# The stores of the gates and of the tokens' order move into the branch of the general path

## The chip, the cores and the metric

The kernel runs on one core of a Trainium2 chip. The metric is the device time of one execution in microseconds (us). TensorE (PE in the rows) multiplies matrices, VectorE (DVE), ScalarE (ACT) and GpSimd (POOL) work on tiles, and SyncE (SP) issues most of the DMAs. Each engine has a sequencer of its own (PEq, DVEq, ACTq, POOLq, SPq) that runs its stream of instructions; PEld stands for TensorE's weight loads.

## The reference

Three layers in a row, all with float32 inputs and outputs. A decay attention of 2 x 8 heads, 768 positions and head size 64 gives 1536 rows `x` of 512. A mixture of 8 experts follows, in which each row goes to one expert:

```python
logits = x @ w_gate
expert_idx = np.argmax(logits, axis=1)
...
gate_w = probs[np.arange(N), expert_idx]
...
    h = np.maximum(xe @ w1[e], 0.0)
    ye = h @ w2[e]
    out[mask] = gate_w[mask, None] * ye
```

Here `w1[e]` is 512 x 1024 and `w2[e]` 1024 x 512. A gated layer ends it, with 1536 inner columns: `sigmoid(x @ w_gate) * (x @ w_val) @ w_out`.

## The kernel before, in words

Every float32 matrix of the two later layers is split into two float16 halves (`hi` and `lo`), and a product is three float16 matmuls. The stages follow one another in the program:

1. Attention, with routing woven into it (lines 264 to 666). Twelve blocks of 128 rows; each block's rows are also stored to DRAM (`rows_d`). The routing gives for every token its expert (`oh_all`), its rank in the expert (`rank_all`) and its gate (`gt_all`, final at some 81 us).
2. The experts (lines 814 to 868). The eight experts are sorted by their token counts, and expert `e` is computed for a fixed number of tokens, `W[e]` of line 47. Its rows are gathered from `rows_d`, multiplied by the gate, transposed and multiplied by `w1` (L827) and `w2` (L855). The result goes into `yh` and `yl`, in order of experts (L863, L864).
3. `order` (line 743, called once at line 869, behind the last expert). TensorE makes a list that holds at each place the token that stands there (L746), and VectorE copies it to `oidx` (L747). SyncE stores the gates to `gate_d` in two DMAs (L749, one for each batch) and `oidx` to `list_d` (L751).
4. The general path (lines 876 to 932). It is for experts with more tokens than `W[e]`. `further` (line 753) counts how many more rounds each expert needs; the largest count is read into a register of every engine at line 842 (`mxv`), and `tc.If(mxv > 0)` at line 876 runs two nested loops. In them GpSimd loads pieces of `list_d` (L885, L886) and gathers rows from `rows_d` and gates from `gate_d`, and TensorE multiplies in float32. Nothing else reads `gate_d` and `list_d`.
5. The gated layer (lines 935 to 980). `gv_ps` (L956) holds `x @ w_gate` and `x @ w_val` in turn, 864 matmuls of 512 columns; sigmoid, product and split follow on ScalarE and VectorE (L960 to L965); `o_ps` (L975) multiplies by `w_out`. GpSimd writes the rows to their tokens' places by the list in SBUF, `oidx` (L979).

The order is written out by hand: the tile framework is told not to reorder (`manual_schedule`), so each engine runs its instructions as the program issues them, and only the semaphores are put in by the framework. Weights of the gated layer come by SyncE in pieces of 1 MB into two buffers (`wload`, L150). Each is turned from its double-precision words to float32 and split, one small step at a time, wherever the program calls `work64`; the next piece can be loaded once VectorE has read the buffer (L219). The If is no part of this order: the framework treats its body as a block, and each engine meets the branch in its own stream.

Of the kernel before, what the change touches and what calls it, by code (L numbers as in the profile page):

```python
# [32 lines left out]
def kernel(  # L33
# [15 lines left out]
    nc = tc.nc  # L49
    B, H, S, D = q.shape  # L50
# [3 lines left out]
    L = 128  # L54
# [41 lines left out]
    gt_all = const.tile([128, NT, 1], F32, name="gt_all")  # L96
    acc = const.tile([128, E], F16, name="acc")
    gidx = const.tile([128, 2, E], I32, name="gidx")
    oidx = const.tile([128, NT], I32, name="oidx")
# [4 lines left out]
    gate_d = dram.tile([NTOK, 1], F32, name="gate_d")  # L104
    list_d = dram.tile([NTOK, 1], I32, name="list_d")
# [141 lines left out]
    def bank(kind, shape, name):  # L247
        turns[kind].append(turns[kind].pop(0))
        tag, bufs = turns[kind][-1]
        return ps.tile(shape, F32, tag=tag, bufs=bufs, name=name)  # L250
# [13 lines left out]
    with ExitStack() as actx:  # L264
# [366 lines left out]
        t = NT - 2  # L631
# [42 lines left out]
    with ExitStack() as mctx:  # L674
# [68 lines left out]
        def order(P, R):  # L743
            ops = bank("b", [128, NT], "o_idx")
            for t in range(NT):
                nc.tensor.matmul(ops, lhsT=P[:, t], rhs=R[:, t], start=(t == 0), stop=(t == NT - 1))  # L746
            nc.vector.tensor_copy(oidx, ops)  # L747
            for b in range(B):
                nc.sync.dma_start(out=gate_d[b * S:(b + 1) * S, :].rearrange("(k p) o -> p k o", p=L),  # L749
                                  in_=gt_all[:, b::B])  # L750
            nc.sync.dma_start(out=list_d[:, :].rearrange("(t p) o -> p (t o)", p=128), in_=oidx)  # L751

        def further():

# [59 lines left out]
        for e in range(E):  # L814
# [31 lines left out]
            for dp in range(KD // 2):  # L846
# [19 lines left out]
                if e < E - 1 or dp == 0:  # L866
                    weights()
            freed[0] = 4 * e + 3
        order(*PR)

    ectx.close()


    with ExitStack() as octx:
        ox_p = octx.enter_context(tc.tile_pool(name="ox", bufs=1))
        with tc.If(mxv > 0):  # L876
            with tc.For_i(0, E, 1) as e:
                nxe = nc.values_load(tab[0:1, bass.ds(e + 2 * E, 1)], min_val=0, max_val=NTOK)
                end = nc.values_load(tab[0:1, bass.ds(e + E, 1)], engines=(ET.DVE, ET.Activation, ET.Pool),
# [2 lines left out]
                with tc.For_i(0, nxe, 1) as i:  # L882
# [6 lines left out]
                    for r, n in ((0, 128), (1, CO - 128)):  # L889
                        nc.gpsimd.indirect_dma_start(  # L890
                            out=xg[0:n, r, :], out_offset=None, in_=rows_d[:, :],
                            in_offset=IndirectOffsetOnAxis(ap=wi[0:n, r:r + 1], axis=0))
                        nc.gpsimd.indirect_dma_start(
                            out=gw[0:n, r:r + 1], out_offset=None, in_=gate_d[:, :],
# [23 lines left out]
                    for dp in range(KD // 2):  # L918
                        w = ox_p.tile([128, KF, 256], F32, tag="ow", name="ow2")
                        nc.gpsimd.dma_start(  # L920
                            out=w, in_=moe_w2[bass.ds(eo, 1), :, dp * 256:(dp + 1) * 256].rearrange(
                                "o (f p) d -> p (o f) d", p=128))
# [12 lines left out]
    with ExitStack() as gctx:  # L935
# [7 lines left out]
        for a in range(KF2 // 4):  # L943
            wg, wv = NC1 + 2 * a, NC1 + 2 * a + 1
            for c2 in range(2):
                for g in range(NG):
                    ts = slice(g * 512, (g + 1) * 512)
                    for f in range(4 * a + 2 * c2, 4 * a + 2 * c2 + 2):
                        fs = slice((f % 4) * 128, (f % 4) * 128 + 128)
                        banks = []  # L950
                        for w in (wg, wv):
                            need(w, c2)
                            p = bank("a", [128, 512], "gv_ps")
# [14 lines left out]
        for t in range(NT):  # L968
            tsl = slice(t * 128, (t + 1) * 128)
            op = bank("b", [128, DM], "o_ps")  # L970
            for f in range(KF2):
# [8 lines left out]
                out=out, out_offset=IndirectOffsetOnAxis(ap=oidx[:, t:t + 1], axis=0), in_=osb, in_offset=None)  # L980
# [30 lines left out]
```

## Time and profile before

| | |
|---|---|
| median of 3 runs | 529.22 us (529.05, 529.22, 531.6) |
| the profiled execution | 530.62 us |
| its span, first to last instruction | 529.0 us |
| TensorE busy in it | 506.9 us (96%) |
| VectorE, ScalarE, GpSimd busy | 306.7, 222.5, 68.3 us |
| TensorE's granted clock, mean | 0.984 |
| DMA | 72.29 MB in 70592 packets, 43338 of them under 512 B |

All times within the execution are counted from the start of the span. [...] "L876" is line 876 of the kernel. A busy time of TensorE contains the pipelining of its matmuls, so that groups overlap. The 16 DMA engines serve several queues: q1 carries what SyncE issues, q0 what GpSimd issues, q8 and q14 carry code for the engines.

### The profile page before, as it was taken

To read this page: it belongs to the slowest core of one execution; us is meant where nothing else is said; L and a number is where in the kernel's file an instruction comes from. 1 tells how busy PE (TensorE), PEld (TensorE's weight loads), DVE (VectorE), ACT (ScalarE), POOL (GpSimd) and SP (SyncE) were. 2 spreads that over 40 slices of the span, in tenths; PEclk is the share of its full clock that TensorE was granted. 3 is DMA by queue.
4 is the path that set the end of the run, shared out by engine and by line. 5 is a ranking of instruction groups with operands and counts; after the bars stand their busy time and mean duration, and the time that the engine had idled before them with its cause. 6 is when DMAs were issued, how large, how long until landed. Compare 5 with 4: busy or idle time off the path is not lost.

```text
span 529.0 us, 9790 instructions
## 1 busy us (share of the span) xinstructions
PE 506.9 (96%) x4013; PEld 340.5 (64%) x4014; DVE 306.7 (58%) x505; ACT 222.5 (42%) x328; POOL 68.3 (13%) x78
## 2 busy tenths in 40 slices
PE   7999998999999999957999999999999999999995
PEld 6888877999999999953444444444444444444442
DVE  5556867979977987741777757677766620000000
ACT  3554642865876787430343433443344310000000
POOL 3676403301200100000000000000000001101101
PEclk9999999999999999987999999999999999999998
DMA  9999865775989885240233222342231001011011
GB/s 171 215 245 268 270 232 184 237 272 168 338 281 314 280 274 187 83 82 1 79 111 128 81 79 81 95 145 79 81 110 51 0 1 40 21 40 41 24 37 40
DMA packets 70592, 72.29 MB, mean 137 GB/s; under 512 B 43338, under 2 KB 43338, under 8 KB 70544
## 3 DMA queue, kind: packets, MB, share of 16 engines
q1 hardware_dynamic: 68192, 65.05, 41.1%
q0 software_dynamic: 2208, 6.57, 3.6%
q8 instruction: 33, 0.54, 0.5%
q14 instruction: 15, 0.12, 0.1%
q10 hardware_dynamic: 144, 0.00, 0.0%
HBM read 65.31 MB, written 6.30 MB: 135 GB/s over the span
## 4 chain that ended last, share of the span: by engine, by line
PE 52%; issue 1%; DMA 1%; POOLq 0%; ACT 0%; ACTq 0%
PE gv_ps L956 36%; PE o_ps L975 16%; DMA out_dram<-osb,oidx 1%; POOLq L1006 0%; ACT osb L978 0%; ACTq L978 0%; POOLq L979 0%
## 5 line engine op out<-in xcount | busy, mean ns | idle before, releaser
L956 PEld LDWEIGHTS <-hi 128*128 128x128 f16 x576 | 56.6, 98 | 77.6 <-issue 10.6
L171 DVE SCALAR_TENSOR_TENSOR lo<-st,hi 128x1024 f16<-128x1024 f32 x64 | 77.9, 1234 | 13.5 <-ACT hi L170 13.3
L956 PE MATMUL gv_ps<-yh,hi 128*128 128x512 f16 x288 | 74.7, 382 | 8.8 <-PEq L876 8.8
L956 PE MATMUL gv_ps<-yh,lo 128*128 128x512 f16 x288 | 74.8, 382 | 0.0
L956 PE MATMUL gv_ps<-yl,hi 128*128 128x512 f16 x288 | 74.4, 381 | 0.0
L170 ACT ACTIVATE hi<-st 128x1024 f16<-128x1024 f32 x64 | 66.2, 1053 | 3.5 <-DMA st<-in_moe_w_dram 3.4
L855 PE MATMUL y_ps<-hl,hi 128*128 128x224 f16 (+6 forms) x256 | 64.6, 253 | 0.3 <-DVE hl L831 0.3
L855 PE MATMUL y_ps<-hh,hi 128*128 128x224 f16 (+6 forms) x256 | 64.6, 253 | 0.0
L855 PE MATMUL y_ps<-hh,lo 128*128 128x224 f16 (+6 forms) x256 | 64.6, 253 | 0.0
L979 POOL DMA_INDIRECT out_dram<-osb,oidx x12 | 11.7, 974 | 336.0 <-ACT osb L978 336.0
L975 PE MATMUL o_ps<-hi,uh 128*128 128x512 f16 x144 | 54.6, 379 | 0.0
L975 PE MATMUL o_ps<-lo,uh 128*128 128x512 f16 x144 | 54.6, 379 | 0.0
L975 PE MATMUL o_ps<-hi,ul 128*128 128x512 f16 x144 | 54.6, 379 | 0.0
L964 ACT CAST uh<-u 128x512 f16<-128x512 f32 x36 | 22.2, 618 | 70.4 <-DVE u L963 70.4
L956 PEld LDWEIGHTS <-lo 128*128 128x128 f16 x288 | 28.4, 99 | 34.6 <-issue 1.1
L975 PEld LDWEIGHTS <-uh 128*128 128x128 f16 x288 | 28.2, 98 | 34.0
L855 PEld LDWEIGHTS <-hi 128*128 128x128 f16 x512 | 47.7, 98 | 0.2
L827 PEld LDWEIGHTS <-hi 128*128 128x128 f16 x512 | 46.4, 98 | 1.2 <-issue 1.1
L978 ACT ACTIVATE osb<-o_ps 128x512 f32<-128x512 f32 x12 | 7.2, 597 | 85.3 <-PE o_ps L975 85.3
L963 DVE SCALAR_TENSOR_TENSOR u<-gv_ps,sg 128x512 f32<-128x512 f32 x36 | 24.7, 687 | 30.2 <-PE gv_ps L956 25.2
L965 DVE TENSOR_TENSOR ul<-u,uh 128x512 f16<-128x512 f32 x36 | 24.9, 692 | 24.6 <-ACT uh L964 24.6
L827 PE MATMUL h_ps<-xh,hi 128*128 128x224 f16 (+6 forms) x256 | 33.5, 253 | 0.3 <-ACT xh L706 0.2
(168 smaller groups left out, 712.6 us busy)
## 6 DMA issues: line engine op xcount, KB each, us to landing
st<-in_moe_w_dram SPq DMA_DIRECT2D x64, 512.0 KB, 5.6
st<-in_moe_w_gate_dram SPq DMA_DIRECT2D x6, 1024.0 KB, 5.3
st<-in_moe_w_val_dram SPq DMA_DIRECT2D x6, 1024.0 KB, 5.1
st<-in_moe_w_out_dram SPq DMA_DIRECT2D x6, 1024.0 KB, 4.9
q<-in_q_dram SPq DMA_DIRECT2D x12, 256.0 KB, 4.5
k<-in_k_dram SPq DMA_DIRECT2D x12, 256.0 KB, 4.9
v<-in_v_dram SPq DMA_DIRECT2D x12, 256.0 KB, 5.9
rows_d<-X SPq DMA_DIRECT2D x12, 256.0 KB, 4.1
```

The costliest lines, as they stand in the source:

```text
L170: nc.scalar.activation(out=hi, in_=w, func=AF.Copy, scale=SW)
L171: return lambda: nc.vector.scalar_tensor_tensor(out=lo, in0=w, scalar=SW, in1=hi, op0=ALU.mult, op1=ALU.subtract)
L827: nc.tensor.matmul(hp[:, j], lhsT=lw[w][:, c, fs], rhs=rx[:, c], start=(c == 0 and m == 0), stop=(c == KD - 1 and m == 2))
L855: nc.tensor.matmul(yp[:, j], lhsT=lw[w][:, f % 4, ds], rhs=rh[:, f], start=(f == 0 and m == 0), stop=(f == KF - 1 and m == 2))
L956: nc.tensor.matmul(p, lhsT=lw[w][:, c, fs], rhs=ry[:, c, ts], start=(c == 0 and m == 0), stop=(c == KD - 1 and m == 2))
L963: nc.vector.scalar_tensor_tensor(out=u, in0=banks[1], scalar=SU, in1=sg, op0=ALU.mult, op1=ALU.mult)
L964: nc.scalar.copy(uh[:, f, ts], u)
L965: nc.vector.tensor_tensor(ul[:, f, ts], u, uh[:, f, ts], op=ALU.subtract)
L975: nc.tensor.matmul(op, lhsT=lu[:, f, tsl], rhs=rw[w][:, f % 4, :], start=(f == 0 and m == 0), stop=(f == KF2 - 1 and m == 2))
L978: nc.scalar.activation(out=osb, in_=op, func=AF.Copy, scale=1.0 / (SX * SW * SW * SY * SW * SU * SW))
L979: nc.gpsimd.indirect_dma_start(out=out, out_offset=IndirectOffsetOnAxis(ap=oidx[:, t:t + 1], axis=0), in_=osb, in_offset=None)
```

## The change

Four lines leave the end of `order` and stand, unchanged, at the start of the If's body. `oidx` is still made in `order`.

```diff
             nc.vector.tensor_copy(oidx, ops)
-            for b in range(B):
-                nc.sync.dma_start(out=gate_d[b * S:(b + 1) * S, :].rearrange("(k p) o -> p k o", p=L),
-                                  in_=gt_all[:, b::B])
-            nc.sync.dma_start(out=list_d[:, :].rearrange("(t p) o -> p (t o)", p=128), in_=oidx)
...
         with tc.If(mxv > 0):
+            for b in range(B):
+                nc.sync.dma_start(out=gate_d[b * S:(b + 1) * S, :].rearrange("(k p) o -> p k o", p=L),
+                                  in_=gt_all[:, b::B])
+            nc.sync.dma_start(out=list_d[:, :].rearrange("(t p) o -> p (t o)", p=128), in_=oidx)
             with tc.For_i(0, E, 1) as e:
```

## Rows read from the trace of the kernel before

**Rows 1.** The chain that ended last, in order of time: start, us, what.

```profile
241.10 0.19 issue
241.30 188.72 PE gv_ps L956 x864
```

**Rows 2.** TensorE's waits, whole span: us in total, times, longest.

```profile
PE gv_ps L956 <- PEq L876: 8.8, 1, 8.8
```

**Rows 3.** Timeline 230.5 to 262: start, us, engine, line; in brackets idle before.

```profile
232.02 0.45 PE L746 MATMUL o_idx<-R,P 128*128 128x12 f16 x12
...
232.73 0.54 DVE L864 SCALAR_TENSOR_TENSOR yl<-y_ps,yh 128x368 f32 x1 [1.27 <-ACTq L876]
...
241.30 1.86 PE L956 MATMUL gv_ps<-yh,hi 128*128 128x512 f16 x4 [8.83 <-PEq L876]
...
246.17 0.60 ACT L960 ACTIVATE sg<-gv_ps 128x512 f32<-128x512 f32 x1 [12.00 <-PE gv_ps L956]
```

**Rows 4.** Line 876: ns min/median/max, then first and last start in us.

```profile
L876 POOLq EVENT_SEMAPHORE  x5: 17/43/43, 175.9 to 182.6; - x5
...
L876 PEldq COMPARE_BRANCH  x1: 9262/9262/9262, 231.6 to 231.6; - x1
L876 ACTq COMPARE_BRANCH  x1: 45/45/45, 232.2 to 232.2; - x1
L876 DVEq COMPARE_BRANCH  x1: 72/72/72, 232.7 to 232.7; - x1
L876 SPq COMPARE_BRANCH  x1: 53/53/53, 233.8 to 233.8; - x1
```

**Rows 5.** DMA queues, 233.3 to 233.5: packets that start there, MB, share of 16 engines.

```profile
q8 instruction: 1, 0.02, 124.7%
```

**Rows 6.** DMA queues, 180 to 200.

```profile
q8 instruction: 2, 0.03, 0.6%
```

**Rows 7.** DMA queues, whole span.

```profile
q8 instruction: 33, 0.54, 0.5%
```

**Rows 8.** DMA packets, 228 to 245.

```profile
DMA packets 3651, 1.10 MB, mean 65 GB/s; under 512 B 3136, under 2 KB 3136, under 8 KB 3648
```

**Rows 9.** Windows: length, five engines' busy us, granted clock, DMA share, GB/s.

```profile
230.00:232.50 2.50, 2.47 (x40) 2.37 (x37) 1.46 (x3) 0.83 (x2) 0.00 (x0) 1.00 0.97 359
...
236.00:239.50 3.50, 0.00 (x0) 0.00 (x0) 0.00 (x0) 0.00 (x0) 0.00 (x0) 0.50 0.28 1
239.50:241.00 1.50, 0.00 (x0) 0.00 (x0) 0.00 (x0) 0.00 (x0) 0.00 (x0) 0.50 0.04 0
...
235.00:235.50 0.50, 0.00 (x0) 0.00 (x0) 0.00 (x0) 0.00 (x0) 0.00 (x0) 0.80 0.19 1
...
245.50:246.00 0.50, 0.50 (x4) 0.25 (x3) 0.00 (x0) 0.00 (x0) 0.00 (x0) 0.95 0.00 0
...
74.88:78.29 3.41, 2.75 (x47) 2.53 (x44) 1.32 (x10) 2.07 (x5) 0.00 (x0) 1.00 0.26 97
78.29:81.70 3.41, 3.40 (x47) 3.32 (x47) 2.46 (x19) 2.21 (x3) 1.17 (x1) 0.50 0.00 1
```

**Rows 10.** SyncE's DMA issues, 150 to 300: start, us.

```profile
228.16 0.38 SPq L150 DMA_DIRECT2D st<-in_moe_w_val_dram  x1
228.59 1.09 SPq L749 DMA_DIRECT2D gate_d<-gt_all  x2
...
254.10 0.37 SPq L150 DMA_DIRECT2D st<-in_moe_w_gate_dram  x1
264.44 0.37 SPq L150 DMA_DIRECT2D st<-in_moe_w_val_dram  x1
```

**Rows 11.** SyncE's waits, 228 to 262: us in total, times, longest.

```profile
SPq L150 <- DVE cv L219: 39.4, 3, 19.9
```

**Rows 12.** Line 877, the general path's outer loop.

```profile
nothing on L877; most used: ['L956', 'L827', 'L855', 'L975', 'L395', 'L380', 'L409', 'L443', 'L150', 'L361', 'L340', 'L391', 'L171', 'L701', 'L454', 'L563', 'L170', 'L960', 'L963', 'L293', 'L524', 'L352', 'L863', 'L964', 'L965']
```

**Rows 13.** DMA queues, 241.7 to 245: packets that start there.

```profile
q8 instruction: 1, 0.02, 5.6%
```

## The prediction

> **What bounds the kernel now.** I read the chain that ended last first. It is TensorE alone: gv_ps from 241.30 for 188.72 us and then o_ps, and it begins at 241.10, in the middle of the program, with a gap in front of it [rows 1]. TensorE's waits name that gap: 8.8 us before the first gv_ps matmul, put down to TensorE's own sequencer at L876, the If [rows 2]. So from 241.30 on every microsecond by which TensorE starts earlier is a microsecond off the end, if its operands are there.
>
> The timeline shows who is busy in the gap [rows 3]. TensorE's twelve o_idx matmuls begin at 232.02 and take 0.45, so it is idle from 232.47 to 241.30. Its operands are ready early: the last yl is written at 232.73 + 0.54 = 233.27, and ACT stands idle for 12.00 us before its first sigmoid at 246.17, so from 234.17 on, waiting for gv_ps. Nothing that computes holds TensorE.
>
> The rows of L876 show what does [rows 4]: one compare-and-branch that takes TensorE's sequencer 9262 ns from 231.6, to about 240.85. ACT, DVE and SP branch in 45 to 72 ns, in the same microseconds. So it is no barrier of all engines, and TensorE's branch has a cost that theirs have not. The DMA view says what it is. In 233.3 to 233.5 one packet of instructions (16 KB) starts, and it is put at 124.7% of 16 engines' 0.2 us, so it takes 1.247 x 3.2 = 3.99 us, to about 237.4 [rows 5]. The two that fell in 180 to 200, beside weight loads at 298 GB/s, took 0.006 x 16 x 20 / 2 = 1.0 us each [rows 6], and the mean of all 33 is 0.005 x 16 x 529 / 33 = 1.3 us [rows 7]. TensorE jumps over the general path's matmuls, has to load code, and that load takes three to four times as long as usual.
>
> Beside it lie the stores. From 228 to 245, 3136 packets are under 512 B [rows 8]; the two gate stores (768 words each) and the list store (1536) make 3072 of them, 4 bytes each. The windows show their tail [rows 9]: 359 GB/s up to 232.5 is the 1 MB weight load issued at 228.16, but in 236 to 239.5 the DMA engines are 0.28 busy at 1 GB/s, and from 239.5 only 0.04. TensorE's branch comes free just behind that tail. The clock adds to the gap: granted 0.80 in the half microsecond from 235.0, so it falls within it, 0.50 after, and 0.95 in the half that ends at 246.
>
> **The change, part by part.** (1) SP loses two gate stores (1.09 us of issue, from 228.59 on), the wait for oidx and the list store [rows 10]. Worth nothing by itself: SP's next load goes out at 254.10, after 19.9 us of waiting for DVE [rows 11], and no engine waits for the stores. Nothing but code is queued behind them, for the next data transfer is that of 254.10.
>
> (2) The three stores go into a path that isn't run (no instruction of its loop at L877 shows [rows 12]), so none of their 3072 packets is sent. What they take from TensorE's code load is the term that counts. Without them the wait has three pieces, each bounded:
> - From the branch (231.6) to the packet's start: at most the present 233.4 - 231.6 = 1.8 us; at least some 0.9, since the code packet that follows the present branch's end at 240.85 starts behind 241.7, in a quiet stretch [rows 13]. The 1 MB load is still in flight to about 232.5, so I take 1.4.
> - The packet: 1.0 to 1.3 us [rows 6, 7]; I take 1.0, the two that lay beside weight loads, as this one does.
> - From the packet's end to the branch's: now 240.85 - 237.4 = 3.4 us, with the stores' tail beside it. That is the upper end; the lower is nothing. I take 0.4, since the tail that fills it now is gone.
>
> Sum 2.8 us, with ends at 0.9 + 1.0 = 1.9 and 1.8 + 1.3 + 3.4 = 6.5. To the first matmul come the present 241.30 - 240.85 = 0.45 us. So TensorE starts at 231.6 + 2.8 + 0.45 = 234.85 and **gains 6.45 us** (ends: 7.35 and 2.75). yl at 233.27 is ready before even the early end; ACT is free from 234.17, and its first sigmoid comes now 4.87 us behind TensorE's start. DVE, ACT and SP's loads behind 241 follow TensorE's results, and move with it.
>
> [...]
>
> (3) The clock. [...] With an idle time of 234.85 - 232.47 = 2.4 us the clock either doesn't fall (gain 2.1) or falls as late as it did (gain nothing). The nearest rows: it fell after 2.5 to 3 us of idling here, and by 78.29 even in a stretch with TensorE busy 2.75 of 3.41 us, where the row at 0.50 is 3.41 us long [rows 9]. 2.4 is near the first, so I take a fall, with the price of such a row: 3.4 us at half speed lose 1.7. **Gain 0.4 us** (ends 0 and 2.1).
>
> (4) Added: SP has to square its semaphores on the path not taken, and its branch jumps further. What that costs is seen on POOL, whose DMAs already stand in the If: five semaphore instructions from 175.9 to 182.6, spread over 6.7 us [rows 4]. SP, at its branch by 228.59 + 1.09 = 229.7 even with the gate stores' issue, would be done by 236.4 at the upper end; at the lower end it adds a few short instructions. The cover is the wait up to 254.10, which moves to 247.3: 10.9 us remain. If they didn't suffice, the weight loads would be late next. I take nothing.
>
> Sum: 6.45 + 0.4 = 6.85 us. The profiled execution, 530.62 with a span of 529.0, would take 523.8; it was 1.4 above the median of 529.22, so for the median I say **522.4**.
>
> **Rivals.**
> - *The clock stays up* (chance 0.20): 6.45 + 2.1 = 8.6 us, 520.6. For it: at 235.0 it had not fallen yet, and TensorE is back by then. Against it: the fall by 78.29, with TensorE at work.
> - *The wait is the branch's own* (0.13): the slow packet and the late end come with a jump, and the stores only lie beside them. Then 241.30 stays, and 529.2, or at best some 2 us less. For it: ACT's and SP's branches, among the same stores, take no time, so stores alone delay no branch; and the packet after the branch, when the small packets are over, still took 0.056 x 16 x 3.3 = 3.0 us [rows 13]. Against it: the two of 180 to 200, and the small packets, which thin out at 239.5, just ahead of the branch's end. [...]
> - *SP's bookkeeping holds the weights* (0.04): if SP's counts on the path not taken are squared only behind something later than the landings, its next load is late. It decides from 247.3 on; loads go out 10.3 us apart (254.10, 264.44), so a whole one missed costs 10.3 - 6.85 = 3.5 us: 532.7, slower. Against it: POOL's took 6.7 us, and SP has 17.6.
>
> **How the numbers follow.** The forecast, a start at 234 to 236.5 with a fall of the clock, has 0.63. A measurement of this kernel tells some 0.5% (2.6 us) from no change. Forecast and the first rival are both faster by more; so faster 0.83, the branch's own wait is same, 0.13, SP's is slower, 0.04. The range: downwards the early start without a fall, 7.35 + 2.1 = 9.45, about 519.8; upwards a start at 237.0 with a fall as dear as now, 4.3 us, 524.9. This leaves out the two last rivals and the latest starts, some 0.2.
>
> **What would show it.** Right: L876's branch on TensorE takes 2 to 4 us; the code packet in it some 1 us; no crowd of packets under 512 B between 232 and 240; the wait before gv_ps is 2 to 3.5 us; SP's loads behind 240 are all earlier by the same amount. The granted clock behind 235 decides between forecast and first rival. Wrong: a branch still near 9 us without those packets; a new wait of gv_ps on DVE or a DMA, with SP's load later than 254.

## The result, and the profile after

| | before | after |
|---|---|---|
| median | 530.94 us (13 runs) | 523.29 us (13 runs) |
| lowest, highest | 527.7, 535.63 | 521.39, 527.42 |
| span of the profiled execution | 529.0 us | 521.7 us |
| TensorE's idle time in front of gv_ps | 8.83 us | 3.03 us |
| TensorE's branch at the If | 9262 ns | 3462 ns |

The kernel after is faster: the ratio is 0.9869, with a 95% interval of 0.9844 to 0.9893. One execution of a kernel further down (gates outside) took 667.47 us at a mean granted clock of 0.747; the ratios leave it out. Line 876 of before is line 872 of after.

The rows of that line in the kernel after, with ns min/median/max and first and last start in us:

```profile
L872 SPq EVENT_SEMAPHORE  x4: 17/17/17, 228.1 to 228.4; - x4
L872 SPq COMPARE_BRANCH  x1: 53/53/53, 227.9 to 227.9; - x1
L872 PEldq COMPARE_BRANCH  x1: 3462/3462/3462, 230.9 to 230.9; - x1
L872 ACTq COMPARE_BRANCH  x1: 45/45/45, 231.6 to 231.6; - x1
L872 DVEq COMPARE_BRANCH  x1: 72/72/72, 232.1 to 232.1; - x1
```

Against [rows 4] only TensorE's branch has changed. SP meets the If at 227.9 in place of 233.8, as it no longer waits for oidx, and squares its counts with four instructions of 17 ns: three more than before, done by 228.4.

TensorE's wait in front of gv_ps, from its waits (us in total, times, longest):

```profile
PE gv_ps L956 <- PEq L872: 3.0, 1, 3.0
```

The beginning of the chain that ended last:

```profile
234.65 0.19 issue
234.84 187.94 PE gv_ps L956 x864
```

Two rows of the timeline, the last matmuls ahead of the gap and the first behind it:

```profile
231.37 0.45 PE L746 MATMUL o_idx<-R,P 128*128 128x12 f16 x12
...
234.84 1.87 PE L956 MATMUL gv_ps<-yh,hi 128*128 128x512 f16 x4 [3.03 <-PEq L872]
```

The span's 7.3 us can be laid out with these and [rows 1, 3]. The o_idx matmuls begin 232.02 - 231.37 = 0.65 us earlier, which is scatter of the work ahead (the branch starts at 231.6 before, at 230.9 here, and between 231.3 and 232.0 in those kernels below that have the same work ahead of it). The gap is shorter by 8.83 - 3.03 = 5.80. The gv_ps stage takes 187.94 in place of 188.72, 0.78 less. That is 7.23; what is left, 0.1, comes behind o_ps.

The code load. In the DMA view of the kernel after, the packets from 228 to 245, and the code queue from 231.90 to 231.95:

```profile
DMA packets 531, 1.09 MB, mean 64 GB/s; under 512 B 16, under 2 KB 16, under 8 KB 528
...
q8 instruction: 1, 0.02, 129.2%
```

Of 3136 small packets [rows 8] 16 are left. The code packet starts at 231.9, 1.0 us behind the branch, and takes 1.292 x 16 x 0.05 = 1.03 us, to 232.95, where it took 3.99 [rows 5]. The branch ends at 230.91 + 3.46 = 234.37, 1.4 us behind the packet.

Windows of the kernel after (length, busy us of five engines, granted clock, DMA share, GB/s):

```profile
233.00:234.80 1.80, 0.00 (x0) 0.00 (x0) 0.00 (x0) 0.52 (x1) 0.00 (x0) 0.81 0.00 0
...
234.00:234.50 0.50, 0.00 (x0) 0.00 (x0) 0.00 (x0) 0.00 (x0) 0.00 (x0) 0.60 0.00 0
234.50:237.50 3.00, 2.65 (x7) 1.04 (x8) 0.00 (x0) 0.00 (x0) 0.00 (x0) 0.50 0.02 5
237.50:238.00 0.50, 0.50 (x4) 0.21 (x3) 0.00 (x0) 0.00 (x0) 0.00 (x0) 0.98 0.00 0
```

The DMA share of a window counts packets by where they start. From 233.0 to 234.8 none starts (the code packet is over by 232.95, and one of 8 KB that begins at 232.93 is over by 233.3), and TensorE still waits. In the traces of both kernels the granted clock is 1.00 or 0.50 at any moment, and a number between them is the mean of a window in which it changes: here it reads 0.50 from 234.10 to 237.52, in the kernel before from 235.31 to 245.54. TensorE works from 234.84 to 237.5 at 0.50, 2.7 us, which costs half of that, 1.35; by the same estimate it cost half of 241.30 to 245.5, 2.1 us, before. The lengths of the gv_ps stage agree: 187.94 and 188.72 us, against 186.64 where it runs at 1.00 (branch's place shifted, below), that is 1.30 and 2.08 more.

SyncE's issues, start and us: the next weight load is 7.2 us earlier than that of 254.10 [rows 10].

```profile
227.51 0.38 SPq L150 DMA_DIRECT2D st<-in_moe_w_val_dram  x1
246.87 0.37 SPq L150 DMA_DIRECT2D st<-in_moe_w_gate_dram  x1
```

### The profile page after: what moved, and what is told of

The parts are those of the page before. It is cut to its first block, busy times and chain, and to the rows that moved or that the text cites. A ratio compares the mean times of both kernels' runs of the same rounds, so it can differ in the third digit from the quotient of the medians.

```text
span 521.7 us, 9789 instructions
## 1 busy us (share of the span) xinstructions
PE 504.3 (97%) x4013; PEld 338.8 (65%) x4014; DVE 306.7 (59%) x505; ACT 222.5 (43%) x328; POOL 69.9 (13%) x78
## 4 chain that ended last, share of the span: by engine, by line
PE 52%; issue 1%; DMA 1%; POOLq 0%; ACT 0%; ACTq 0%
PE gv_ps L956 36%; PE o_ps L975 16%; DMA out_dram<-osb,oidx 1%; POOLq L1006 0%; ACT osb L978 0%; ACTq L978 0%; POOLq L979 0%
## 5 line engine op out<-in xcount | busy, mean ns | idle before, releaser
L170 ACT ACTIVATE hi<-cv 128x1024 f16<-128x1024 f32 x18 | 19.0, 1055 | 35.0 <-DVE cv L219 35.0
```

Of the source, the lines that this page charges most:

```text
L170: nc.scalar.activation(out=hi, in_=w, func=AF.Copy, scale=SW)
```

## The experiments

Each is compared with runs of the kernel before on its own chip. "Branch" is TensorE's compare-and-branch at the If; in the first row it is from a second profile of the same kernel.

| kernel | median us | ratio to before | branch ns |
|---|---|---|---|
| gates outside | 530.43 | 0.9982 (0.9949 to 1.0016) | 9422 |
| list outside | 525.13 | 0.9887 (0.9855 to 0.9918) | 3842 |
| rows of 48 bytes | 524.29 | 0.9888 (0.9855 to 0.9922) | 3682 |
| 4 bytes, into SBUF | 526.82 | 0.9936 (0.9900 to 0.9971) | 4482 |
| gates twice | 533.27, one run | | 12082 |
| no branch | 519.47 | 0.9773 (0.9757 to 0.9789) | none |
| short jump | 520.6 | 0.9804 (0.9780 to 0.9829) | 357 |
| load earlier | 524.3 | 0.9863 (0.9841 to 0.9886) | 3322 |
| branch's place shifted | 518.35 | 0.9766 (0.9723 to 0.9810) | 450 |
| after, again | 525.2 | 0.9883 (0.9837 to 0.9928) | 3422 |
| before, shifted | 518.64 | 0.9772 (0.9728 to 0.9816) | 362 |

### Which of the stores: gates outside, list inside

```diff
             nc.vector.tensor_copy(oidx, ops)
+            for b in range(B):
+                nc.sync.dma_start(out=gate_d[b * S:(b + 1) * S, :].rearrange("(k p) o -> p k o", p=L),
+                                  in_=gt_all[:, b::B])
...
         with tc.If(mxv > 0):
-            for b in range(B):
-                nc.sync.dma_start(out=gate_d[b * S:(b + 1) * S, :].rearrange("(k p) o -> p k o", p=L),
-                                  in_=gt_all[:, b::B])
```

> The two gate stores stand in order() as before, the list store stays in the If. Theory (TensorE's code load waits for the 4-byte stores that are in flight on its DMA engine): the gates' 1536 packets are sent just ahead of the branch, so they carry most of it: branch 6 to 9 us (before 9.3, after 3.5), the code packet again 2 to 4 us long, time 527 to 531. Rival 1 (it is the list store, the one whose tail reaches to 240): branch 3.3 to 4 us, time 522 to 524. Rival 2 (it is SP's wait for oidx and the late SP branch, not the packets): as rival 1, for SP doesn't wait here.

530.43 us, no faster than before: the two gate stores alone carry the whole loss. The rows below are from a second profile of the same kernel, of 530.83 us.

> The first experiment again (gates outside, list inside), for a profile at the full clock: branch 8 to 9.5 us, in three pieces as before, 1.8 to the packet's start, 3 to 4 for the packet, 3 to 4 from its end.

The branch's row there:

```profile
L875 PEldq COMPARE_BRANCH  x1: 9422/9422/9422, 231.7 to 231.7; - x1
```

Its DMA view, packets and code queue from 233.4 to 233.6, then the packets from 233.6 to 241:

```profile
DMA packets 105, 0.02 MB, mean 84 GB/s; under 512 B 104, under 2 KB 104, under 8 KB 104
...
q8 instruction: 1, 0.02, 142.1%
...
DMA packets 1, 0.01 MB, mean 1 GB/s; under 512 B 0, under 2 KB 0, under 8 KB 0
```

Its window from 233.5 to 241:

```profile
233.50:241.00 7.50, 0.00 (x0) 0.00 (x0) 0.00 (x0) 0.76 (x1) 0.00 (x0) 0.64 0.01 1
```

The code packet starts 1.8 us behind the branch, as in the kernel before, takes 1.421 x 3.2 = 4.5 us, to 238.0, and the branch ends 3.0 us later at 241.1. Now look at the packets from 233.6 on and at the window. All gate packets have been sent by 233.6, and from then on only one packet starts, of 8 KB, until the branch is over. (The share of 0.01 doesn't contain the code packet, which starts at 233.47, ahead of the window.) So TensorE's code load isn't held by packets that still have to be sent. What takes the time comes behind them. In the trace of the kernel before, whose gate packets start from 232.56 to 233.58, the semaphores of the two gate stores are raised 16 times each, from 236.4 to 242.6: 2.8 to 9.1 us behind the last of these packets, on both sides of the branch's end at 240.9. So the stores' reports come long after their packets, and TensorE doesn't wait for all of their reports. Expected were 3 to 4 us for the code packet, so 4.5 is a miss there.

### The list alone

The same edit the other way round: the list store in `order`, the gates in the If.

> The list store stands in order() as before, with SP's wait for oidx; the gate stores stay in the If. Theory, if the packets that are there when the code load begins decide: the list store is issued some 1.8 us behind TensorE's branch, after the code packet has started, so it can hold only the load's end: branch 3.5 to 5 us, time 522 to 526. Rival 1 (the list store's tail carries the wait) and rival 2 (SP's wait): branch 7 to 9 us, time 527 to 531.

The branch:

```profile
L873 PEldq COMPARE_BRANCH  x1: 3842/3842/3842, 231.5 to 231.5; - x1
```

The code queue from 235.9 to 236.1, from the DMA view:

```profile
q8 instruction: 1, 0.02, 120.0%
```

The branch is within 0.4 us of after's: the list goes out too late to hold this code packet, which starts at 232.8 and takes 0.146 x 16 x 0.5 = 1.2 us (SP meets the If, right behind the list store, at 233.7), and SP's wait for oidx, which is back here, costs nothing. Behind the list's 1536 packets it is the next code packet that is slow, 1.2 x 3.2 = 3.84 us from 236.0 on, but TensorE's branch is over by 235.3, ahead of it.

### Few rows, or 4 bytes into SBUF

Both are the kernel after with three more stores in `order`, read by nobody. First, in rows of 48 bytes to DRAM (two tiles `wide_g`, one `wide_l`, each 128 x 12):

```diff
             nc.vector.tensor_copy(oidx, ops)
+            nc.sync.dma_start(out=wide_g[0][:, :], in_=gt_all.rearrange("p k o -> p (k o)"))
+            nc.sync.dma_start(out=wide_g[1][:, :], in_=gt_all.rearrange("p k o -> p (k o)"))
+            nc.sync.dma_start(out=wide_l[:, :], in_=oidx)
```

> The kernel after, and in order() three more stores to scratch DRAM of the same bytes and more, in rows: twice all the gates and once the list, each 128 packets of 48 bytes, 384 packets in place of 3072. Theory (the number of small writes to DRAM): branch 3.5 to 4.5 us, time 522 to 525. Rival (any store in flight, or any DMA issued by SP there, holds the code load): branch 8 to 9 us, time 527 to 531.

Second, 3072 pieces of 4 bytes as before, but into SBUF:

```diff
             nc.vector.tensor_copy(oidx, ops)
+            for b in range(B):
+                nc.sync.dma_start(out=gate_s[:, b::B], in_=gt_all[:, b::B])
+            nc.sync.dma_start(out=list_s[:, :, 0], in_=oidx)
```

> The kernel after, and in order() three more copies in pieces of 4 bytes, 3072 packets as before, but into SBUF tiles that nothing reads. If the mere number of packets holds the code load, branch 6 to 9 us and 527 to 531; if it is the slow landing of 4-byte writes in DRAM, branch 3.5 to 4.5 us and 522 to 525. I lean to the landing in DRAM: in the kernel before the gate packets were read within 1 us, at 9 ns each, and it was their landings that came up to 9 us later.

The branch with rows of 48 bytes:

```profile
L877 PEldq COMPARE_BRANCH  x1: 3682/3682/3682, 231.4 to 231.4; - x1
```

The branch with 4 bytes into SBUF:

```profile
L877 PEldq COMPARE_BRANCH  x1: 4482/4482/4482, 231.9 to 231.9; - x1
```

The DMA view of the latter: packets from 228 to 245, the code queue from 233.7 to 233.9, and the gate copies' issue (KB each, us to landing):

```profile
DMA packets 3651, 1.10 MB, mean 65 GB/s; under 512 B 3136, under 2 KB 3136, under 8 KB 3648
...
q8 instruction: 1, 0.02, 34.7%
...
gate_s<-gt_all SPq DMA_DIRECT2D x2, 3.0 KB, 5.2
```

Stores to DRAM as such don't hold the branch: 384 packets of 48 bytes (256 of them, the gates', are issued ahead of it) add 0.2 us. The same 3136 small packets as in [rows 8] add 1.0 us when they go to SBUF, and 5.8 when they go to DRAM. The 1.0 is a delay of the start: the code packet begins at 233.7 to 233.9, some 1.9 us behind the branch, as with the gates to DRAM, but takes only 0.347 x 3.2 = 1.1 us, and the branch ends 4.48 - 1.9 - 1.1 = 1.5 us behind it. The gate copies, issued at 228.9 and 229.7, have landed 5.2 us after their issue. So with 1536 such packets ahead the code packet starts 0.8 to 0.9 us later, wherever they write; the packet's length and what follows it grow only when they write to DRAM. Whether that is because the writes are so many or because each is so small is not separated here: the rows of 48 bytes change both. The time of the second, 526.82 us, is in neither of the expected ranges: it is 2.5 us above that with rows of 48 bytes, where the branch explains 0.8, and the rest stays open.

### More of them

```diff
+            for b in range(B):
+                nc.sync.dma_start(out=gate_d2[b * S:(b + 1) * S, :].rearrange("(k p) o -> p k o", p=L),
+                                  in_=gt_all[:, b::B])
```

behind the gate stores of the kernel before, to scratch DRAM.

> The kernel before, and in order() a second pair of gate stores, to scratch DRAM, right behind the first: 1536 more 4-byte packets ahead of the code load. Theory (start of the code packet: its engine works off some 96 packets of 9 ns for each pair of gate stores, 0.9 us; then the packet and its report wait for the landings in DRAM): branch 11 to 15 us, packet's start at 2.6 us or more behind the branch's, time 533 to 538. If landings overlap or another bound holds, branch 9 to 10 us.

The branch:

```profile
L880 PEldq COMPARE_BRANCH  x1: 12082/12082/12082, 231.3 to 231.3; - x1
```

The code queue from 233.0 to 233.2, from the DMA view:

```profile
q8 instruction: 1, 0.02, 135.3%
```

Twice the gates make the branch 2.8 us longer, in the range expected. But the packet starts at 1.8 us, not later than before, and takes 4.3 us, hardly more than 3.99; the growth lies behind the packet's end (243.4 - 237.4 = 6 us). The expected later start is a miss: twice the packets ahead don't hold the start longer.

### What the rest of the branch is

Without the If and its body (the general path is left out):

> The kernel after without the If and its body; this leaves out the general path, which isn't run on this data. What is left of the branch's cost: TensorE's idle time of 3.0 us in front of gv_ps goes to 0.5 us or less and the clock doesn't fall there (1.3 us). Theory: span 4 us below that of after, 517 to 518, time 518 to 520. Rival (another wait takes the branch's place, by ACT's table load at 234.2 or yl): idle 1 to 2.5 us, time 520 to 523.

The timeline:

```profile
233.31 0.45 PE L746 MATMUL o_idx<-R,P 128*128 128x12 f16 x12
233.62 1.02 PE L891 MATMUL gv_ps<-yh,hi 128*128 128x512 f16 x4
```

gv_ps begins 0.31 us behind the first o_idx matmul, and no other wait takes the branch's place: 519.47 us. Then the kernel after with the gated layer's weights worked on earlier:

```diff
-    N64, N64G = 57, 3
+    N64, N64G = 55, 3
```

> The kernel after with N64 = 55 in place of 57: the gated layer's weights are worked on two slots earlier, so the 1 MB load that is in flight at the branch (227.5 to 232.5) goes out some 3.8 us earlier and is over by 229. What is left of the branch, 3.46 us, has three pieces: 1.0 to the packet's start, 1.0 for it, 1.4 from its end. If the load takes part in the first or the last, the branch falls to 2 to 2.9 us and the time by 0.5 to 2; if not, 3.2 to 3.5 us and the same time, 522.5 to 524.

The branch:

```profile
L872 PEldq COMPARE_BRANCH  x1: 3322/3322/3322, 232.9 to 232.9; - x1
```

SyncE's last load ahead of it, from the timeline:

```profile
226.35 0.38 SPq L150 DMA_DIRECT2D st<-in_moe_w_val_dram  x1
```

The window in which it waits:

```profile
232.90:236.00 3.10, 0.91 (x20) 0.82 (x18) 0.62 (x2) 1.76 (x2) 0.00 (x0) 1.00 0.03 8
```

The load went out 227.51 - 226.35 = 1.2 us earlier only, but the branch comes 2.0 us later too, so that the load is over and the DMA engines are 0.03 busy while TensorE waits. The branch still takes 3.32 us: this is the jump's own price, with next to nothing beside it. The clock stays at 1.00 in this window, though TensorE idles 2.9 us in front of gv_ps, and its mean over the execution is 0.999, where the profile of after has 0.996.

### Where the jump lands

In the next, the sums over `c` and `f` of the general path's two products are cut to their first term, which makes TensorE's part of it shorter (part of the general path is left out).

```diff
-                                for c in range(KD):
-                                    nc.tensor.matmul(hp[:, j], lhsT=w[:, c, f * 128:(f + 1) * 128], rhs=xf[:, c],
-                                                     start=(c == 0), stop=(c == KD - 1))
+                                nc.tensor.matmul(hp[:, j], lhsT=w[:, 0, f * 128:(f + 1) * 128], rhs=xf[:, 0],
+                                                 start=True, stop=True)
```

and the like for `yp`.

> The kernel after with a general path that holds 20 matmuls of TensorE in place of 72 (the sums over c and f are cut to their first term; this leaves out part of the general path, which isn't run). If the jump's length makes the code load, as the short branches of ACT and DVE let one suppose, TensorE's branch takes 0.1 us or less, or still 3.5 if a page of code begins between; time 518 to 520 in the first case, 523 to 524 in the second. I can't say which: it hangs on where in its 16 KB the branch stands. The code packet of 224 should be the last ahead of the branch in either case.

The branch:

```profile
L872 PEldq COMPARE_BRANCH  x1: 357/357/357, 231.3 to 231.3; - x1
```

The branch is nearly free, though it costs more than the 0.1 us expected at best. To tell the jump's length from its place, the whole general path comes back, and only the code ahead of it gets shorter: the warm-up matmuls of the routing, 66 of 128 columns, become 17 of 512.

```diff
-    NB, WARM = 3, (30, 14, 8, 20, 24)
+    NB, WARM = 3, (30, 4, 2, 5, 6)
...
+    wide16 = const.tile([128, 512], F16, name="wide16")
...
-        warm(WARM[1], tag="tr", bufs=3)
+        warm(WARM[1], wide16, tag="tr", bufs=3)
```

> The kernel after with the whole general path, and the branch at another place in TensorE's code: of the warm-up matmuls in the routing, 66 of 128 columns become 17 of 512 (the same columns, 49 pairs of instructions less ahead of the branch). The jump is as long as in after. Theory (the branch waits only where its target lies beyond the code already loaded; a code packet of 16 KB is some 256 instructions, the one of 224 is the last ahead of the branch, and the short jump of the last experiment stayed inside it): moved back by 98 instructions the target falls into loaded code, branch 0.1 to 0.5 us, time 519.5 to 521, as with the short jump. Rival (the length alone decides, any jump so long loads code): branch 3.3 to 3.6 us and the time of after.

> The kernel after, unchanged, on the same chip as the others of this call, to compare them with: 523 to 524, branch 3.4 to 3.6 us.

The 256 instructions to a code packet can be read in the gated layer of the kernel before: from 320.3 to 348.0 one packet of the code queue starts, and TensorE has 130 matmuls and 129 weight loads in that window.

The shifted kernel's branch:

```profile
L875 PEldq COMPARE_BRANCH  x1: 450/450/450, 229.7 to 229.7; - x1
```

What is left of the wait in front of gv_ps:

```profile
PE gv_ps L959 <- ACTq L875: 0.4, 1, 0.4
```

The beginning of its chain:

```profile
230.91 0.16 issue
231.07 186.64 PE gv_ps L959 x864
```

Its window behind that:

```profile
232.00:237.00 5.00, 5.00 (x25) 2.28 (x24) 0.48 (x1) 0.92 (x2) 0.00 (x0) 1.00 0.01 3
```

It is the place: the same jump takes 0.45 us, and TensorE waits 0.4 us, now for ScalarE's last yh. The runs were 518.12 to 518.7 us, those of after on the same chip 523.54 to 525.75. The clock stays at 1.00, and the gv_ps stage takes 186.64 us, 1.3 less than in the first profile of after. This kernel beats both, with the general path whole, and its time is a little under the expected 519.5. The profile of after on the same chip has a longer fall of the clock than the first one, as its chain shows:

```profile
235.85 189.40 PE gv_ps L956 x864
```

Of the 7.5 us between the two spans (524.2 and 516.7), 2.5 are the gap, 2.8 the stage; the remaining 2.2 lie ahead of the branch, which comes at 229.7 and not at 232.0. In the two shifted kernels it comes at 229.7 and 230.0, in the nine profiles with the old warm-up and the same work ahead at 230.9 to 232.0, so some 1 to 2 us seem to belong to the changed warm-up and not to the jump. Only this one shift was tried.

### The stores without a code load

The same shift in the kernel before, with all three stores outside the If.

> The kernel before, with all three stores outside the If, and the same shift of the branch's place as e9. If the stores cost time only by way of TensorE's code load, they now cost nothing, for there is no load to hold: branch 0.1 to 0.5 us, time as e9, 519.5 to 521.5. If they hold something else too (the weight load, the next code packet, the gated layer's start), 522 to 528.

The branch:

```profile
L879 PEldq COMPARE_BRANCH  x1: 362/362/362, 230.0 to 230.0; - x1
```

The DMA view, packets from 226 to 245 and the code queue from 231.7 to 231.9:

```profile
DMA packets 3661, 1.14 MB, mean 60 GB/s; under 512 B 3136, under 2 KB 3136, under 8 KB 3657
...
q8 instruction: 1, 0.02, 118.6%
```

The beginning of the chain:

```profile
231.23 0.17 issue
231.40 186.71 PE gv_ps L959 x864
```

518.64 us, 0.3 from the kernel with the stores inside (expected 519.5 to 521.5). All 3136 small packets are sent, and a code packet, the next one, again takes 1.186 x 3.2 = 3.8 us beside them. But TensorE doesn't wait for that one: its branch is over at 230.4, 1.4 us before the packet starts at 231.8, and gv_ps starts at 231.40 and takes 186.71 us (186.64 with the stores inside). So, within 0.3 us, the stores cost time in one way alone, by way of a code load that TensorE waits for.

## Why the prediction was right, point by point

- **The number.** 522.4 us was foreseen, with a range of 519.8 to 524.9, and 523.29 measured. The forecast was counted from 529.22, the median of three runs; 13 runs of the kernel before give 530.94, so the gain is 7.65 us where 6.85 was foreseen. In the two profiles the terms give 5.80 + 0.78 = 6.58. That this is so near 6.85 is partly luck: the gap shrank by 0.65 less than foreseen and the stage by 0.4 more, and 0.65 of scatter ahead of the branch is not the change's.
- **The bound.** That every microsecond of an earlier gv_ps comes off the end held: the gap and the stage explain 6.6 of the span's 7.3 us, and the weight loads behind followed (246.87 against the 247.3 of the text).
- **SP's own savings are worth nothing**: shown by the list alone, where SP waits for oidx again and TensorE's branch stays within 0.4 us.
- **The code load** was named as what the stores hold, and the gates outside, the gates twice and the two shifted kernels show it. The rival by which the wait is the branch's own falls with the first of these; the 3.3 to 3.5 us that are its own stay, where the forecast had 2.8.
- **The pieces.** Foreseen 1.4 + 1.0 + 0.4 = 2.8 us, measured 1.0 + 1.03 + 1.4 = 3.46. The term that was mis-sized is the last: "I take 0.4, since the tail that fills it now is gone". Without any store it is 1.4, and with the DMA engines idle (share 0.00 from 233.0 to 234.8). The first was too long by 0.4. So TensorE gained 5.80 us in place of 6.45, between the ends of 2.75 and 7.35.
- **Which tail.** The text put the branch's end "just behind that tail", the windows of 0.28 busy to 239.5. Those packets are the list's, and the list alone costs 0.4 us; the gates outside give the same 3.0 us behind the packet with the DMA engines idle. So the tail that comes just ahead of the branch's end is not what holds it. What holds it goes out with the gates' stores and lasts beyond their packets, as their reports do (236.4 to 242.6 in the trace of before). By which way they hold the load is not shown; that it is their writing in DRAM is an inference from the runs: the piece was 3.4 us with the gates to DRAM in before, 3.0 with the gates outside, and is 1.4 to 1.5 without them or with them going to SBUF. That the piece might fall to nothing, the forecast's lower end, is out: 1.4 us are there without such writes.
- **The clock** fell in the profiled execution, as forecast, for a shorter stretch: 0.78 us gained in the gv_ps stage, 0.4 foreseen (ends 0 and 2.1). The 2.1 us that the forecast takes for a clock that stays up stand in no row; the runs show 188.72 - 186.64 = 2.08 us in their place, the stage before against the stage with the clock at 1.00. The size of the gain is one draw. In the second profile of the same kernel the stage takes 189.40 us, 0.7 more than before the change. The rival in which the clock stays up isn't out either: with 2.9 us of idling it stayed up in the profile of the load earlier (1.00 in the window around the branch, mean clock 0.999), and one of the 13 runs of after has that mean clock too, at 521.39 us. With the jump's place shifted it came true.
- **SP's bookkeeping** takes 0.5 us, four instructions, and waits for no load in flight. The upper end of 6.7 us, taken over from GpSimd's rows, doesn't apply; the cover was never needed.

## What to carry to other kernels

TensorE, jumping over the general path, took 3.3 to 3.5 us in one place and 0.45 in another, and with TensorE the bound that wait went into the time. Look at the duration of each engine's branch in the profile: keep stores like these (1536 writes of 4 bytes to DRAM, 5.8 us on the branch) from going out just ahead of a branch that takes microseconds, and see whether fewer instructions ahead of it, or in the block, make it short (3462 to 357 ns with 20 matmuls in place of 72 in the block, to 450 with 98 instructions less ahead of it). Here the latter was worth more than the change itself (12.1 us from the kernel before, 1 to 2 of them perhaps the warm-up's, against 7.65), and it made the stores harmless.

## What the runs showed of the hardware that was not expected

- With 1536 stores of 4 bytes to DRAM ahead of it, a code load ends some 7.5 us after the last of their packets (233.6 to 241.1). Its own packet takes 4.4 us of these, and in the last 3.0 no packet is in flight, so a view of packets doesn't show what is waited for; the stores' own reports do point to it: in the trace of the kernel before they come 2.8 to 9.1 us behind the stores' last packet. The same pieces into SBUF leave the packet at 1.1 us.
- TensorE's branch costs 3.3 us with DMA engines 0.03 busy; its code packet takes 0.292 x 3.2 = 0.93 us of these, from 233.9 on, and the last 1.4 us show in no packet. What they are stays open.
- The price of the same jump is 0.36 to 0.45 us or 3.3 to 3.5, depending on 98 instructions ahead of it. That the boundary is one of loaded code is the author's inference; it fits that in the kernel before, shifted, no code packet is awaited (the next one starts at 231.8, 1.4 us after the branch has ended). How far ahead code is loaded was not varied; in the kernel after, the awaited packet of 231.9 is followed by one at 235.1 and then by none on that queue until 258.0. Not measured was the time with the general path running, which this data doesn't need.
